# Constant products on TensorE in the first tiles, and a start that is loaded and converted in pieces

## The chip, the cores and the metric

The kernel runs on one core of one Trainium2 chip. The metric is the device time of one execution in microseconds (us), and the profile is that of one execution taken by the hardware profiler. The engines are called PE (TensorE), DVE (VectorE), ACT (ScalarE), POOL (GpSimd) and SP (SyncE, which here only issues transfers).

## What is computed

An attention whose scores are cut off close to each row's maximum feeds a chain of matrix products, whose result feeds a mixture of eight experts. Sizes: 4 batches x 8 heads, 576 tokens, 64 per head; 2304 tokens of 512 features; inner width 1024. The four weights of the middle part arrive as 64-bit floats.

```python
scores = scale * np.matmul(q, k.transpose(0, 1, 3, 2))
thresh = np.max(scores, axis=-1, keepdims=True) - tau
scores = np.where(scores >= thresh, scores, -1000000000.0)
attn = np.exp(scores - np.max(scores, axis=-1, keepdims=True))
attn = attn / (np.sum(attn, axis=-1, keepdims=True) + 1e-09)
x = np.matmul(attn, v)
...
h = (x @ w1) * (x @ w2) @ w3
x = h @ w_out
...
for e in range(E):
    out += P[:, e:e + 1] * (np.maximum(x @ w1[e], 0.0) @ w2[e])
```

## The kernel before, in words

The order of the instructions on each engine is written out by hand; there is no scheduler. `attention` walks over 16 pairs of heads with nine tiles of 128 query rows each, so 144 tiles, and a step `s` of its main loop does one stage of several tiles. The letters of `ORDER = "mSTqelVoyifgsrRcxtXvwz"` name the stages in the order in which a step writes them: `m` the mask of tile s (DVE, L160), `S` the scores of tile s+2 (PE, L140), `T` and `e` the transposes of tile s-1 and their way out of PSUM (PE L185, ACT L190), `q` and `l` the same for the tails of three tiles (L196, L201), `r` and `R` the preparation of the next pair of heads, `c` and `z` the conversion of 64-bit weights, `x`, `t` and `X` row maximum (DVE L145), threshold (ACT L148) and exponential (ACT L153) of tile s+2, `v` the products with the values for tile s-5 (PE L227), `y` and `i` their scaling and the reciprocals (DVE), `V` and `o` the transposes back and the copies into x for the group of s-10, `w` products of `w3` and `w_out`, and `f` the copy of a finished block of those (ACT L437, `w34o`) with its store.

The scores have two buffers (`bufs=2` in `scores`). So the scores of tile s+2 wait for the mask of tile s, the mask waits for the exponential, and that waits for the row maximum.

Queries and keys are split in two parts for exact products: `kh` (ACT, L116) and the rest `kl` (DVE or POOL, L119), `qs` (ACT L108, lower half finished by DVE L112). The pieces of a pair of heads are named by `prep(n, part)`. Head 0 of pair 0 is done ahead of the loop, and `PREP` gives the steps of the later pairs.

`W34` converts the 40 chunks of 64-bit weights in four pieces each (`to_f32`, DVE L455 to L463, POOL L464 and L465). A step takes 2 pieces for s < RAMP = 4 and `CONVERT[s % 18]` pieces later, and `mms` issues up to `PRODUCTS[s % 18]` of the 192 products of converted chunks per step, once their chunks are there.

The second half of the kernel, `Moe`, is opened in the first step from 144 on in which all 192 products are done and copied out:

```python
if s >= NT and k.moe is None and fill.done():
    early.close()
    k.moe = Moe(k)
```

Its tiles take the memory that `early.close()` gives back, so its first instructions wait until the last store of `w34o` has read it. They sum and split x (DVE L590 and L598, ACT L597) and load and split the first weights (SP L526, POOL L543 to L555); a DVE instruction `u` (L636) is the first that needs sums of the new products.

Of the kernel before, what the change touches and what calls it, by code (L numbers as in the profile page):

```python
# [9 lines left out]
F32 = mybir.dt.float32  # L10
F32R = mybir.dt.float32r
AF = mybir.ActivationFunctionType
ALU = mybir.AluOpType
# [6 lines left out]
B, H, S, D = 4, 8, 576, 64  # L20
DM, DFF, E = 512, 1024, 8
NTOK = B * S
NP = B * H // 2
# [10 lines left out]
CONVERT = (1, 1, 1, 1, 1, 1, 1, 1, 0, 1, 1, 2, 2, 1, 1, 2, 1, 1)  # L34
# [2 lines left out]
PREP = {1: (0, 4), 2: (2, 1), 4: (3,), 5: (6,), 7: (8, 5), 8: (9, 7)}  # L37
PD = 2
SHARE = 2.0
RAMP = 4  # L40
CHUNKS = "oowoooo33o3o33ww3ww3333wwww3w33w3ww3ww3w"


def f32(ap):
    return ap.bitcast(F32)
# [6 lines left out]
def attention(k):  # L52

    tc, nc = k.tc, k.nc
    early, late = ExitStack(), ExitStack()
    pool = late.enter_context(tc.tile_pool(name="att", bufs=1, side="right"))
    psum = late.enter_context(tc.tile_pool(name="attp", bufs=1, space=bass.MemoryType.PSUM, side="right"))
    epool = early.enter_context(tc.tile_pool(name="atte", bufs=1))
    psums = early.enter_context(tc.tile_pool(name="atts", bufs=1, space=bass.MemoryType.PSUM))

    k.ident = pool.tile([128, 128], F32, name="ident")
    make_identity(nc, k.ident)
    NT = 9 * NP
    last = pool.tile([128, 65], F32, name="last")
# [3 lines left out]
    thr = pool.tile([128, 18], F32, name="thr")  # L68
# [4 lines left out]
    raws, sets = {}, {}  # L73

    def load(n, i):
        if n >= NP:
            return
        t = epool.tile([128, 2, S], F32, tag=f"r{i}", name=f"r{i}_{n}", bufs=2)
        raws[n, i] = t
        if n:  # L80
            fetch(n, i, slice(0, 2))

    def fetch(n, i, h):
        for half in range(2):
            nc.sync.dma_start(raws[n, i][64 * half:64 * half + 64, h], k.qk[n, :, 2 * i + h.start:2 * i + h.stop])

    def load_v(n):
        if n >= NP:
            return
        rv = pool.tile([128, 2, 5, D], F32, tag="rv", name=f"rv{n}", bufs=2)  # L90
        nc.sync.dma_start(rv, k.vv[n])
        raws["v", n] = rv

    def prep(n, part):
        if n >= NP:
            return
        rq, rk = raws[n, 0], raws[n, 1]
        if n not in sets:
            qs = epool.tile([128, QW], F32R, tag="qs", name=f"qs{n}", bufs=2)
            kh = epool.tile([128, 2, S], F32R, tag="kh", name=f"kh{n}", bufs=2)  # L100
            kl = epool.tile([128, 2, S], F32R, tag="kl", name=f"kl{n}", bufs=2)
            sets[n] = (qs, kh, kl)
            nc.gpsimd.memset(f32(qs[:, S:S + 128]), 0.0)
        qs, kh, kl = sets[n]
        qcol = (slice(0, S), slice(S + 128, QW))
        if part in (0, 1):
            h = part
            nc.scalar.activation(qs[:, qcol[h]], rq[:, h], AF.Copy, scale=0.125)  # L108
        elif part in (2, 3, 8, 9):
            h, o = part % 2, 0 if part < 4 else 288  # L110
            dst = qs[64:128, qcol[h].start + o:qcol[h].start + o + 288]
            nc.vector.scalar_tensor_tensor(  # L112
                out=dst, in0=rq[64:128, h, o:o + 288], scalar=0.125, in1=f32(dst), op0=ALU.mult, op1=ALU.subtract)
        elif part in (4, 5):
            h = part - 4
            nc.scalar.activation(kh[:, h], rk[:, h], AF.Copy)  # L116
        elif part in (6, 7):
            h = part - 6
            (nc.gpsimd if n or h else nc.vector).tensor_tensor(out=kl[:, h], in0=rk[:, h], in1=f32(kh[:, h]), op=ALU.subtract)  # L119

    spool, ppool, tpool, outs = {}, {}, {}, {}

    def scores(s):
        if s >= NT:
            return
        n, t = divmod(s, 9)
        qs, kh, kl = sets[n]
        ps = psums.tile([128, 2, 512], F32, tag="s", name=f"s{s}", bufs=2)
        spool[s] = ps
        if t == 4:  # L130
            todo = [(512, 0), (640, 1)]
        elif t < 4:
            todo = [(128 * t, 0)]
        else:
            todo = [(QW - S + 64 + 128 * (t - 5), 1)]
        for c in range(2):
            cols = slice(288 * c, 288 * c + 288)
            ops = [(q0, h, kk) for q0, h in todo for kk in (kh, kl)]
            for i, (q0, h, kk) in enumerate(ops):
                nc.tensor.matmul(ps[:, c, 0:288], lhsT=qs[:, q0:q0 + 128], rhs=kk[:, h, cols],  # L140
                                 start=i == 0, stop=i == len(ops) - 1)

    def rowmax(s):
        ps = spool[s]
        nc.vector.tensor_reduce(out=nmx[:, s % 18:s % 18 + 1], in_=ps[:, :, 0:288], axis=AX.XY, op=ALU.max, negate=True)  # L145

    def thresh(s):
        nc.scalar.activation(thr[:, s % 18:s % 18 + 1], nmx[:, s % 18:s % 18 + 1], AF.Identity, bias=k.ntau, scale=-1.0)  # L148

    def expo(s):  # L150
        e = pool.tile([128, 2, 288], F32, tag="e", name=f"e{s}", bufs=2)
        spool[s] = (spool[s], e)
        nc.scalar.activation(e, spool[s][0][:, :, 0:288], AF.Exp, bias=nmx[:, s % 18:s % 18 + 1], scale=1.0)  # L153

    def mask(s):
        ps, e = spool.pop(s)
        g, i = divmod(s, 3)
        if i == 0:
            ppool[g] = pool.tile([128, 3, S + 4], F32, tag="p", name=f"p{g}", bufs=3)
        nc.vector.scalar_tensor_tensor(out=ppool[g][:, i, 0:S].rearrange("p (a b) -> p a b", a=2), in0=ps[:, :, 0:288],  # L160
                                       scalar=thr[:, s % 18:s % 18 + 1], in1=e, op0=ALU.is_ge, op1=ALU.mult,
                                       accum_out=ssum[:, s % 18:s % 18 + 1])
# [40 lines left out]
    def vsum(n):  # L203

        rv = raws["v", n]
        ps = psum.tile([128, 512], F32, tag="tt", name=f"vs{n}", bufs=1)
        for i in range(5):
            r = 128 if i < 4 else 64
            nc.tensor.matmul(ps[0:65, 0:128], lhsT=last[0:r], rhs=rv[0:r, :, i], start=i == 0, stop=i == 4)
        nc.scalar.activation(rv[64:65, :, 4], ps[64:65, 0:128].rearrange("p (a b) -> p a b", a=2), AF.Copy)  # L210
# [39 lines left out]

    load(0, 1)
    load(0, 0)
    for h in range(2):
        fetch(0, 1, slice(h, h + 1))
        fetch(0, 0, slice(h, h + 1))
    nc.sync.dma_start(k.ntau, k.tau.to_broadcast([128, 1]))
    nc.scalar.activation(thr[:, 0:1], k.ident[:, 0:1], AF.Exp)
    fill = W34(k, epool, psum)
    load(1, 0)
    load(1, 1)  # L260
    for part in (4, 6, 0, 2):
        prep(0, part)
    nc.scalar.mul(k.ntau, k.ntau, -1.0)
    load_v(0)
    scores(0)
    scores(1)
    for s in range(2):
        rowmax(s)
        thresh(s)
        expo(s)  # L270
    prep(0, 8)
    prep(0, 5)
    prep(0, 7)

    def parts(s, which):
        n, t = divmod(s, 9)
        for part in PREP.get(t, ())[which]:
            prep(n + 1, part)

    def tiles(f, d):  # L280

        return lambda s: f(s - d) if 0 <= s - d < NT else None

    def groups(f, d):

        return lambda s: f((s - d) // 3) if (s - d) % 3 == 0 and 0 <= s - d < NT else None

    steps = {
        "m": tiles(mask, 0), "S": tiles(scores, -2), "x": tiles(rowmax, -2), "t": tiles(thresh, -2), "X": tiles(expo, -2),
        "T": tiles(transp, 1), "e": tiles(evac, 1), "g": groups(flags, 1), "s": groups(sums, 3), "i": groups(inverse, 5),  # L290
        "q": groups(tails, 3), "l": groups(tail_out, 3), "v": tiles(pv, 5), "y": groups(scale, 8),
        "V": groups(back, 10), "o": groups(x_out, 10), "f": lambda s: fill.out(),
        "c": lambda s: fill.convert(s, 2 if s < RAMP else CONVERT[s % 18]), "z": lambda s: fill.convert(s, 0),
        "r": lambda s: parts(s, slice(0, 1)), "R": lambda s: parts(s, slice(1, 9)), "w": lambda s: fill.mms(s)}
    ahead = iter(())
    for s in range(NT + 19):
        n, t = divmod(s, 9)
# [3 lines that stand above are left out]
            ahead = k.moe.run()  # L301
        for what in ORDER:
            if what in steps:
                steps[what](s)
        if s < 2:
            for part in ((1, 3), (9,))[s]:
                prep(0, part)
        if n < NP and t in (2, 4):
            load(n + 2, t // 2 - 1)
        if n < NP and t == 2:  # L310
            vsum(n)
        if n < NP and t == 6:
            load_v(n + 1)
        if k.moe:
            next(ahead)
# [618 lines left out]
```

## Time and profile before

| | before |
|---|---|
| median of 3 timed runs | 2296.33 us (2295.28 to 2297.43) |
| the profiled execution, device time | 2291.91 us |
| its span, first to last instruction | 2290.1 us |
| PE busy | 2228.0 us, 97% of the span |
| DVE, ACT, POOL busy | 1261.5, 971.5, 1055.0 us |

The device time of the profiled execution is 1.8 us above its span, and the median of the timed runs lies 4.4 us above it. Starts in the rows are microseconds from the start of the span. Of each row of a timeline the columns are: start, duration, engine, line, operation, output<-inputs, shapes, number of merged instructions, and in brackets the idle time ahead of it with what ended it.

### The profile page before, as it was taken

How to read it: one execution, taken by the hardware profiler on the slowest of the kernel's cores; microseconds unless marked ns; L12 is line 12 of the kernel's file. 1: busy time of each engine (PE TensorE's matmuls, PEld its weight loads, DVE VectorE, ACT ScalarE, POOL GpSimd, SP SyncE). 2: the span in 40 equal slices, each digit the busy share in tenths (PEclk: the TensorE clock that was granted, in tenths of full speed). 3: DMA queues.
4: the chain of work that ended last, by engine and by line, in shares of the span. 5: the costliest groups of instructions: out<-in, count | busy, mean ns of one | idle time of the engine just before them, and what ended most of it. 6: DMA issues, size and time to landing. Idle time of an engine off the chain costs nothing.

```text
span 2290.1 us, 32049 instructions
## 1 busy us (share of the span) xinstructions
PE 2228.0 (97%) x12544; PEld 2034.3 (89%) x12544; DVE 1261.5 (55%) x2207; ACT 971.5 (42%) x1805; POOL 1055.0 (46%) x997
## 2 busy tenths in 40 slices
PE   6999999989999999999999999999999999999999
PEld 5899999888989888999999999999999999999998
DVE  7888888665554555544444634444445544444444
ACT  6877877643222433333333433333333343333332
POOL 4654555385110444444455644444445544444442
PEclk9999999989999999999999999999999999999999
DMA  5434443165444212112212212212212212211211
GB/s 144 119 104 123 130 122 118 50 243 206 151 168 174 78 56 74 66 64 74 71 59 74 102 56 74 74 56 74 74 56 74 102 57 72 74 63 68 74 67 44
DMA packets 57432, 213.37 MB, mean 93 GB/s; under 512 B 7105, under 2 KB 7105, under 8 KB 57281
## 3 DMA queue, kind: packets, MB, share of 16 engines
q1 hardware_dynamic: 57280, 211.33, 27.0%
q8 instruction: 98, 1.61, 0.3%
q14 instruction: 54, 0.43, 0.1%
HBM read 185.61 MB, written 25.69 MB: 92 GB/s over the span
## 4 chain that ended last, share of the span: by engine, by line
PE 69%; DVE 1%; issue 0%; ACT 0%; POOL 0%; DVEq 0%; ACTq 0%
PE ye L679 36%; PE py L609 19%; PE px L609 14%; DVE xl L598 0%; PE py L758 0%; DVE c L653 0%; PE px L758 0%; DVE c L664 0%; DVE prob L796 0%; ACT xh L597 0%; DVE acc L733 0%; POOL w1l L553 0%; DVE hl L675 0%; POOL w1l L550 0%; DVE small L793 0%
## 5 line engine op out<-in xcount | busy, mean ns | idle before, releaser
L679 PE MATMUL ye<-w2h,hl 128*128 128x512 f32 x1152 | 452.0, 392 | 0.0
L679 PE MATMUL ye<-w2h,hh 128*128 128x512 f32 x1152 | 451.4, 392 | 0.0
L679 PE MATMUL ye<-w2l,hh 128*128 128x512 f32 x1152 | 450.5, 391 | 0.0
L674 ACT ACTIVATE hh<-c 128x384 fp32r<-128x384 f32 x288 | 151.4, 526 | 611.4 <-DVE c L653 611.3
L555 POOL TENSOR_TENSOR w1l<-wt,w1h 128x1024 fp32r<-128x1024 f32 x104 | 251.7, 2420 | 286.4 <-ACT w1h L552 286.4
L609 PE MATMUL py<-xh,w1h 128*128 128x384 f32 x960 | 323.7, 337 | 8.4 <-DVE c L653 3.6
L609 PE MATMUL py<-xl,w1h 128*128 128x384 f32 x960 | 323.0, 336 | 3.5 <-DVE xl L598 3.5
L609 PE MATMUL py<-xh,w1l 128*128 128x384 f32 x960 | 322.0, 335 | 0.4 <-POOL w1l L555 0.4
L550 POOL TENSOR_TENSOR w1l<-raw,w1h 128x256 fp32r<-128x256 f32 x104 | 79.4, 764 | 479.0 <-ACT w1h L544 463.7
L609 PE MATMUL px<-xh,w1h 128*128 128x384 f32 x720 | 242.8, 337 | 5.5 <-ACT p L633 2.8
L679 PEld LDWEIGHTS ye<-w2l,hh 128*128 128x128 f32 x1152 | 216.3, 188 | 32.4
L679 PEld LDWEIGHTS ye<-w2h,hl 128*128 128x128 f32 x1152 | 216.2, 188 | 32.4
L609 PE MATMUL px<-xl,w1h 128*128 128x384 f32 x720 | 242.2, 336 | 2.7 <-DVE xl L598 2.7
L609 PE MATMUL px<-xh,w1l 128*128 128x384 f32 x720 | 242.1, 336 | 0.0
L679 PEld LDWEIGHTS ye<-w2h,hh 128*128 128x128 f32 x1152 | 216.3, 188 | 24.1 <-ACT x L705 0.2
L609 PEld LDWEIGHTS py<-xh,w1h 128*128 128x128 f32 x960 | 180.4, 188 | 33.1 <-DVE c L653 6.4
L609 PEld LDWEIGHTS py<-xl,w1h 128*128 128x128 f32 x960 | 180.3, 188 | 23.2 <-DVE xl L598 5.3
L636 DVE TENSOR_TENSOR u<-py,p 128x384 f32<-128x384 f32 x120 | 66.7, 556 | 216.0 <-PE py L609 212.1
L609 PEld LDWEIGHTS py<-xh,w1l 128*128 128x128 f32 x960 | 180.3, 188 | 0.9 <-POOL w1l L555 0.9
L543 POOL TENSOR_TENSOR wt<-raw 128x512 f32<-128x512 f32 x104 | 140.5, 1351 | 87.2 <-DMA raw<-in_e 61.0
L675 DVE SCALAR_TENSOR_TENSOR hl<-c,hh 128x384 fp32r<-128x384 f32 x288 | 165.1, 573 | 9.3
L674 ACT ACTIVATE hh<-px 128x384 fp32r<-128x384 f32 x96 | 47.2, 492 | 272.5 <-PE px L609 272.5
(138 smaller groups left out, 4393.9 us busy)
## 6 DMA issues: line engine op xcount, KB each, us to landing
raw<-in_e SPq DMA_DIRECT2D x192, 512.0 KB, 4.0
r<-in_qk SPq DMA_DIRECT2D x60, 288.0 KB, 5.8
wraw<-in_w SPq DMA_DIRECT2D x32, 512.0 KB, 4.0
w1h<-w_kept SPq DMA_DIRECT2D x16, 896.0 KB, 4.9
w1l<-w_kept SPq DMA_DIRECT2D x16, 896.0 KB, 6.8
w_kept<-w1h SPq DMA_DIRECT2D x8, 896.0 KB, 7.3
w_kept<-w1l SPq DMA_DIRECT2D x8, 896.0 KB, 8.2
raw<-w SPq DMA_DIRECT2D x12, 512.0 KB, 3.5
```

The costliest lines, as they stand in the source:

```text
L543: nc.gpsimd.tensor_tensor(out=t[:, 0:2], in0=raw[:, 1:3], in1=raw[:, 0:2], op=ALU.subtract)
L550: nc.gpsimd.tensor_tensor(out=wl[:, 0], in0=raw[:, 0], in1=f32(wh[:, 0]), op=ALU.subtract)
L555: nc.gpsimd.tensor_tensor(out=wl[:, 3:7], in0=t, in1=f32(wh[:, 3:7]), op=ALU.subtract)
L609: self.nc.tensor.matmul(out, lhsT=w[:, wi, o], rhs=x[xi][:, d], start=n == 0 and not adds, stop=n == 5, skip_group_check=True)
L636: tt(out=self.u2, in0=py, in1=self.p1, op=ALU.add)
L674: nc.scalar.activation(hi, src, AF.Relu)
L675: self.later.append(lambda: nc.vector.scalar_tensor_tensor(out=lo, in0=src, scalar=0.0, in1=f32(hi), op0=ALU.max, op1=ALU.subtract))
L679: self.queue.append((out.shape[-1], lambda: self.nc.tensor.matmul(out, lhsT=l, rhs=r, start=start, stop=stop, skip_group_check=True)))
```

## The change

A tile `hot` of ones is set by DVE, and `busy(n)` issues n products of 128x512 from it, written to the PSUM buffer that the `w34` products use later. They stand ahead of the first scores (9), behind the scores of tile 1 (7), and at the end of the steps 0 to 11 (1, 5, 6, 6, 5, 4, 4, 3, 3, 2, 2, 2): 59 in all, whose results nobody reads. The first head's keys and queries are loaded in smaller pieces, two of them issued by ACT, and split in halves. The masks of tiles 0 and 1 stand both in step 0, and the second head of pair 0 is prepared ahead of the first conversions. No pieces are converted in the steps 0 and 1, and two in each of the steps 2 to 5.

```diff
--- before.py
+++ after.py
@@ -37,7 +37,8 @@
 PREP = {1: (0, 4), 2: (2, 1), 4: (3,), 5: (6,), 7: (8, 5), 8: (9, 7)}
 PD = 2
 SHARE = 2.0
-RAMP = 4
+RAMP = 6
+BUSY = (1, 5, 6, 6, 5, 4, 4, 3, 3, 2, 2, 2)
 CHUNKS = "oowoooo33o3o33ww3ww3333wwww3w33w3ww3ww3w"
 
 
@@ -59,6 +60,8 @@
     psums = early.enter_context(tc.tile_pool(name="atts", bufs=1, space=bass.MemoryType.PSUM))
 
     k.ident = pool.tile([128, 128], F32, name="ident")
+    hot = epool.tile([128, 128], F32R, name="hot")
+    nc.vector.memset(f32(hot), 1.0)
     make_identity(nc, k.ident)
     NT = 9 * NP
     last = pool.tile([128, 65], F32, name="last")
@@ -91,17 +94,21 @@
         nc.sync.dma_start(rv, k.vv[n])
         raws["v", n] = rv
 
-    def prep(n, part):
-        if n >= NP:
-            return
-        rq, rk = raws[n, 0], raws[n, 1]
+    def operands(n):
+
         if n not in sets:
             qs = epool.tile([128, QW], F32R, tag="qs", name=f"qs{n}", bufs=2)
             kh = epool.tile([128, 2, S], F32R, tag="kh", name=f"kh{n}", bufs=2)
             kl = epool.tile([128, 2, S], F32R, tag="kl", name=f"kl{n}", bufs=2)
             sets[n] = (qs, kh, kl)
             nc.gpsimd.memset(f32(qs[:, S:S + 128]), 0.0)
-        qs, kh, kl = sets[n]
+        return sets[n]
+
+    def prep(n, part):
+        if n >= NP:
+            return
+        rq, rk = raws[n, 0], raws[n, 1]
+        qs, kh, kl = operands(n)
         qcol = (slice(0, S), slice(S + 128, QW))
         if part in (0, 1):
             h = part
@@ -119,6 +126,13 @@
             (nc.gpsimd if n or h else nc.vector).tensor_tensor(out=kl[:, h], in0=rk[:, h], in1=f32(kh[:, h]), op=ALU.subtract)
 
     spool, ppool, tpool, outs = {}, {}, {}, {}
+
+    def busy(n):
+
+        if n:
+            ps = psum.tile([128, 4, 128], F32, tag="w34", name="hot", bufs=1)
+        for i in range(n):
+            nc.tensor.matmul(ps, lhsT=hot, rhs=hot.unsqueeze(1).to_broadcast([128, 4, 128]), start=True, stop=True)
 
     def scores(s):
         if s >= NT:
@@ -250,27 +264,43 @@
 
     load(0, 1)
     load(0, 0)
-    for h in range(2):
-        fetch(0, 1, slice(h, h + 1))
-        fetch(0, 0, slice(h, h + 1))
+    rk, rq = raws[0, 1], raws[0, 0]
+    both = ((nc.sync, slice(0, 64)), (nc.scalar, slice(64, 128)))
+    for eng, half in both:
+        eng.dma_start(rk[half, 0:1], k.qk[0, :, 2:3])
+    for eng, half in both:
+        eng.dma_start(rq[half, 0, 0:288], k.qk[0, :, 0, 0:288])
+    for half in (slice(0, 64), slice(64, 128)):
+        nc.sync.dma_start(rq[half, 0, 288:S], k.qk[0, :, 0, 288:S])
     nc.sync.dma_start(k.ntau, k.tau.to_broadcast([128, 1]))
-    nc.scalar.activation(thr[:, 0:1], k.ident[:, 0:1], AF.Exp)
+    for i in (1, 0):
+        fetch(0, i, slice(1, 2))
+    nc.scalar.activation(thr[:, 0:1], f32(hot)[:, 0:1], AF.Exp)
     fill = W34(k, epool, psum)
     load(1, 0)
     load(1, 1)
-    for part in (4, 6, 0, 2):
-        prep(0, part)
+    busy(9)
+    qs, kh, kl = operands(0)
+    nc.scalar.activation(kh[:, 0], rk[:, 0], AF.Copy)
+    nc.scalar.activation(qs[:, 0:288], rq[:, 0, 0:288], AF.Copy, scale=0.125)
+    nc.vector.tensor_tensor(out=kl[:, 0, 0:288], in0=rk[:, 0, 0:288], in1=f32(kh[:, 0, 0:288]), op=ALU.subtract)
+    prep(0, 2)
+    nc.vector.tensor_tensor(out=kl[:, 0, 288:S], in0=rk[:, 0, 288:S], in1=f32(kh[:, 0, 288:S]), op=ALU.subtract)
+    nc.scalar.activation(qs[:, 288:S], rq[:, 0, 288:S], AF.Copy, scale=0.125)
     nc.scalar.mul(k.ntau, k.ntau, -1.0)
     load_v(0)
     scores(0)
     scores(1)
-    for s in range(2):
-        rowmax(s)
-        thresh(s)
-        expo(s)
+    busy(7)
     prep(0, 8)
-    prep(0, 5)
-    prep(0, 7)
+    rowmax(0)
+    expo(0)
+    thresh(0)
+    rowmax(1)
+    expo(1)
+    thresh(1)
+    for part in (5, 7, 1):
+        prep(0, part)
 
     def parts(s, which):
         n, t = divmod(s, 9)
@@ -286,11 +316,11 @@
         return lambda s: f((s - d) // 3) if (s - d) % 3 == 0 and 0 <= s - d < NT else None
 
     steps = {
-        "m": tiles(mask, 0), "S": tiles(scores, -2), "x": tiles(rowmax, -2), "t": tiles(thresh, -2), "X": tiles(expo, -2),
+        "m": lambda s: [mask(i) for i in ((0, 1) if s == 0 else () if s == 1 or s >= NT else (s,))], "S": tiles(scores, -2), "x": tiles(rowmax, -2), "t": tiles(thresh, -2), "X": tiles(expo, -2),
         "T": tiles(transp, 1), "e": tiles(evac, 1), "g": groups(flags, 1), "s": groups(sums, 3), "i": groups(inverse, 5),
         "q": groups(tails, 3), "l": groups(tail_out, 3), "v": tiles(pv, 5), "y": groups(scale, 8),
         "V": groups(back, 10), "o": groups(x_out, 10), "f": lambda s: fill.out(),
-        "c": lambda s: fill.convert(s, 2 if s < RAMP else CONVERT[s % 18]), "z": lambda s: fill.convert(s, 0),
+        "c": lambda s: fill.convert(s, (0, 0, 2, 2, 2, 2)[s] if s < RAMP else CONVERT[s % 18]), "z": lambda s: fill.convert(s, 0),
         "r": lambda s: parts(s, slice(0, 1)), "R": lambda s: parts(s, slice(1, 9)), "w": lambda s: fill.mms(s)}
     ahead = iter(())
     for s in range(NT + 19):
@@ -302,9 +332,12 @@
         for what in ORDER:
             if what in steps:
                 steps[what](s)
-        if s < 2:
-            for part in ((1, 3), (9,))[s]:
-                prep(0, part)
+        if s < len(BUSY):
+            busy(BUSY[s])
+        if s == 0:
+            prep(0, 3)
+        elif s == 1:
+            prep(0, 9)
         if n < NP and t in (2, 4):
             load(n + 2, t // 2 - 1)
         if n < NP and t == 2:
```

On ACT, at the end of step 0 and in step 1, the rows before are these (`kh0`, `qs0` are the second head of pair 0, `qs1`, `kh1` the first head of pair 1, `cvq`, `cvl` the conversion, `pt0` the transposes of tile 0 on their way out):

```order
L116 ACTIVATE kh0_118<-r1_0_93 128x576
L453 ACTIVATE cvq_158<-wraw0_107 128x512
L454 ACTIVATE cvl_159<-wraw0_107 128x512
L148 ACTIVATE thr_89<-nmx_88,ntau_62 128x1
L153 ACTIVATE e2_166<-s2_151,nmx_88 128x576
L108 ACTIVATE qs0_117<-r0_0_94 128x576
L190 ACTIVATE pt0_184<-t0_179 128x512
L108 ACTIVATE qs1_189<-r0_1_111 128x576
L116 ACTIVATE kh1_190<-r1_1_114 128x576
L148 ACTIVATE thr_89<-nmx_88,ntau_62 128x1
L153 ACTIVATE e3_198<-s3_174,nmx_88 128x576
```

And in the changed kernel:

```order
L123 ACTIVATE kh0_132<-r1_0_95 128x576
L115 ACTIVATE qs0_131<-r0_0_96 128x576
L162 ACTIVATE thr_91<-nmx_90,ntau_62 128x1
L167 ACTIVATE e2_184<-s2_177,nmx_90 128x576
L204 ACTIVATE pt0_199<-t0_194 128x512
L115 ACTIVATE qs1_204<-r0_1_115 128x576
L123 ACTIVATE kh1_205<-r1_1_118 128x576
L162 ACTIVATE thr_91<-nmx_90,ntau_62 128x1
L167 ACTIVATE e3_212<-s3_189,nmx_90 128x576
```

The conversion has left this place and `qs0` stands earlier; `qs1` and `kh1`, which need the second pair's load, still stand ahead of the threshold and the exponential of tile 3.

On PE, the steps 2 to 4 before (`t` transposes, `vs0` the sums over the values, `tt0` tails; runs of equal rows are merged):

```order
L185 MATMUL t1_214<-ident_80,p0_149 128x128 x4
L209 MATMUL vs0_243<-rv0_126,last_85 65x128 x5
L140 MATMUL s5_252<-kh0_118,qs0_117 128x288
L140 MATMUL s5_252<-kl0_119,qs0_117 128x288
L140 MATMUL s5_252<-kh0_118,qs0_117 128x288
L140 MATMUL s5_252<-kl0_119,qs0_117 128x288
L185 MATMUL t2_257<-ident_80,p0_149 128x128 x4
L196 MATMUL tt0_262<-ident_80,p0_149 65x128 x3
L140 MATMUL s6_280<-kh0_118,qs0_117 128x288
```

And in the changed kernel:

```order
L199 MATMUL t1_231<-ident_80,p0_174 128x128 x4
L135 MATMUL hot_255<-hot_81 128x512 x6
L223 MATMUL vs0_265<-rv0_142,last_87 65x128 x5
L154 MATMUL s5_274<-kh0_132,qs0_131 128x288
L154 MATMUL s5_274<-kl0_133,qs0_131 128x288
L154 MATMUL s5_274<-kh0_132,qs0_131 128x288
L154 MATMUL s5_274<-kl0_133,qs0_131 128x288
L199 MATMUL t2_279<-ident_80,p0_174 128x128 x4
L210 MATMUL tt0_284<-ident_80,p0_174 65x128 x3
L135 MATMUL hot_301<-hot_81 128x512 x6
L154 MATMUL s6_309<-kh0_132,qs0_131 128x288
```

Six constant products stand between one tile's transposes and the next tile's scores, in each of these steps.

On PE, from the last products of step 143 on, before (`w34_7` the last block of products, `pv` products with the values, `xt` transposes back):

```order
L426 MATMUL w34_7_5253<-wol_106,w3h38_5512 128x512
L426 MATMUL w34_7_5253<-woh_105,w3l38_5513 128x512
L185 MATMUL t143_5660<-ident_80,p47_5583 128x128 x4
L196 MATMUL tt47_5665<-ident_80,p47_5583 65x128 x3
L227 MATMUL pv46_5652<-rv15_5292,pt139_5565 128x2x64 x4
L227 MATMUL pv46_5652<-rv15_5292,ptt46_5601 128x2x64
L241 MATMUL xt45_5714<-ident_80,xo45_5649 64x128 x3
L227 MATMUL pv46_5652<-rv15_5292,pt140_5599 128x64 x4
L227 MATMUL pv46_5652<-rv15_5292,ptt46_5601 128x64
L227 MATMUL pv47_5735<-rv15_5292,pt141_5623 128x64 x4
```

And in the changed kernel:

```order
L199 MATMUL t143_5737<-ident_80,p47_5654 128x128 x4
L210 MATMUL tt47_5742<-ident_80,p47_5654 65x128 x3
...
L241 MATMUL pv46_5728<-rv15_5363,pt140_5670 128x64 x4
L241 MATMUL pv46_5728<-rv15_5363,ptt46_5672 128x64
L459 MATMUL w34_7_5358<-wol_110,w3h38_5639 128x512
L241 MATMUL pv47_5771<-rv15_5363,pt141_5698 128x64 x4
L241 MATMUL pv47_5771<-rv15_5363,ptt47_5748 128x64
L241 MATMUL pv47_5771<-rv15_5363,pt142_5722 128x64 x4
L241 MATMUL pv47_5771<-rv15_5363,ptt47_5748 128x64
L459 MATMUL w34_7_5358<-woh_109,w3l38_5640 128x512
L255 MATMUL xt46_5783<-ident_80,xo46_5767 64x128 x4
```

The last two of the 192 products have moved from step 143, ahead of the transposes of tile 143, to the steps 145 and 147. The copy `w34o` stands in the step after the last product, and `Moe` opens in the step after that: step 145 before, step 149 now.

## Rows read from the trace of the kernel before

**Rows 1.** Windows: stretch, length, busy us of PE, PEld, DVE, ACT, POOL; clock; DMA share; GB/s.

```profile
10.00:18.00 8.00, 2.84 (x11) 2.54 (x12) 4.96 (x11) 4.34 (x9) 2.35 (x5) 1.00 1.02 277
100.00:400.00 300.00, 292.66 (x2280) 274.99 (x2280) 251.18 (x526) 234.95 (x500) 163.99 (x232) 1.00 0.41 121
```

**Rows 2.** Timeline of PE: starts of scores (s) and sums (vs), tiles 3 to 13.

```profile
16.46 0.58 PE L140 MATMUL s<-kh,qs 128*128 128x288 f32 x1 [3.80 <-DVE p L160]
...
17.55 1.05 PE L185 MATMUL t<-ident,p 128*128 128x128 f32 x4
20.36 0.58 PE L140 MATMUL s<-kh,qs 128*128 128x288 f32 x1 [1.75 <-DVE p L160]
...
23.26 2.38 PE L209 MATMUL vs<-rv,last 128*65 128x128 f32 x10
25.58 0.40 PE L140 MATMUL s<-kh,qs 128*128 128x288 f32 x1
...
31.97 0.44 PE L140 MATMUL s<-kh,qs 128*128 128x288 f32 x1 [2.44 <-DVE p L160]
...
49.17 0.40 PE L140 MATMUL s<-kh,qs 128*128 128x288 f32 x1
```

**Rows 3.** Timeline of PE, the step from the scores of tile 8 to those of tile 9.

```profile
35.69 0.38 PE L140 MATMUL s<-kh,qs 128*128 128x288 f32 x1
...
37.06 1.00 PE L227 MATMUL pv<-rv,pt 128*128 128x64 f32 x8
...
38.10 0.38 PE L140 MATMUL s<-kh,qs 128*128 128x288 f32 x1
```

**Rows 4.** Timeline of DVE: the mask of tile 1, a conversion pass in step 2.

```profile
15.49 0.82 DVE L160 SCALAR_TENSOR_TENSOR p<-s,thr,e 128x576 f32<-128x576 f32 x1
...
20.85 1.40 DVE L455 TENSOR_SCALAR cva<-wraw 128x512 int32<-128x512 int32 x1
```

**Rows 5.** Timeline of ACT: the second pair's keys and the exponential of tile 3.

```profile
19.71 0.67 ACT L116 ACTIVATE kh<-r 128x576 fp32r<-128x576 f32 x1
...
20.47 0.73 ACT L153 ACTIVATE e<-s,nmx 128x576 f32<-128x576 f32 x1
```

**Rows 6.** Timeline of SP: issue of the first loads (start, time of all, count).

```profile
0.72 5.04 SPq L85 DMA_DIRECT2D r<-in_qk  x8
...
7.38 2.39 SPq L85 DMA_DIRECT2D r<-in_qk  x4
9.81 0.58 SPq L91 DMA_DIRECT2D rv<-in_vv  x1
```

**Rows 7.** DMA issues from 9.15 to 9.9: operation, count, KB, us to landing.

```profile
rv<-in_vv SPq DMA_DIRECT2D x1, 320.0 KB, 9.2
r<-in_qk SPq DMA_DIRECT2D x1, 288.0 KB, 9.0
```

**Rows 8.** Timeline of PE: two neighbouring products of 128x512.

```profile
416.48 0.39 PE L426 MATMUL w<-wol,w3h 128*128 128x512 f32 x1
416.71 0.39 PE L426 MATMUL w<-woh,w3l 128*128 128x512 f32 x1
```

**Rows 9.** Timeline of PE from the transposes of tile 143 on.

```profile
451.57 0.60 PE L185 MATMUL t<-ident,p 128*128 128x128 f32 x4
...
453.78 1.00 PE L227 MATMUL pv<-rv,pt 128*128 128x64 f32 x8
...
458.42 1.53 PE L227 MATMUL pv<-rv,pt 128*128 128x64 f32 x8 [3.41 <-DVE rin L179]
```

**Rows 10.** Timeline of ACT where the second half opens.

```profile
453.07 0.59 ACT L437 ACTIVATE w34o<-w 128x512 f32<-128x512 f32 x1
...
455.91 0.84 ACT L597 ACTIVATE xh<-x 128x768 fp32r<-128x768 f32 x1 [1.44 <-DMA w<-w34o]
```

**Rows 11.** Timeline of DVE where the second half opens.

```profile
457.79 0.48 DVE L234 TENSOR_TENSOR xo<-pv,rin 128x128 f32<-128x128 f32 x2
...
474.08 0.54 DVE L636 TENSOR_TENSOR u<-py,p 128x384 f32<-128x384 f32 x1
```

## The prediction

> **What bounds the kernel now.** I read the page first, then the windows by stage, then the timelines of the first 55 us and of the stretch from 440 to 480 us. From 100 to 400 us PE is busy 292.7 of 300 us, DVE 251.2 [rows 1]: the attention is bound by PE there, and a tile that comes earlier or later at 50 us stays so up to step 143. After the opening of the second half the instructions of before and after stand in the same order on all engines. So the change can act in two places only: the first 14 tiles, and the opening.
>
> In the first tiles PE waits. The scores of tile 3 start at 16.46 after 3.80 us of idle time that DVE's mask ended, those of tile 7 at 31.97 after 2.44 us [rows 2]. [...] At the opening a serial chain runs: copy `w34o` at 453.07, its store, first split of x at 455.91 [rows 10], and `u` at 474.08 [rows 11], while PE waits.
>
> **The first tiles, step by step.** The eight loads of the first pair took SP 5.04 us, 0.63 each [rows 6]. With ACT issuing a half, the first keys lie 0.6 us earlier, and splitting in halves adds perhaps as much again. [...] I put tile 0 at 1.4 us earlier; the next gate makes the exact figure unimportant.
>
> The mask of tile 1 started at 15.49 [rows 4] behind two conversion passes, a row maximum and a head's split, and the scores of tile 3 followed 0.97 us behind it [rows 2]. It now stands right behind the mask of tile 0, so tile 3 can start at about 10 and tile 4 at 13.5 instead of 20.36 [rows 2]: 6 to 7 us gained, for the moment.
>
> What is late next is a load. `qs1` and `kh1` stand on ACT ahead of the exponential of tile 3, and `kh1` needs the last of four transfers that SP issued from 7.38 on: issued at 9.2, landed 9.0 us later, at 18.2 [rows 6, 7]. Before, `kh1` started at 19.71 [rows 5], so nobody saw it. SP issues sixteen loads up to `rv0` in both kernels, and the 16 engines were fully busy (share 1.02) from 10 to 18 us [rows 1], so I leave 18.2. From the start of `kh1` to the end of the exponential is 20.47 + 0.73 - 19.71 = 1.49 us [rows 5]: exponential done at 19.75, mask, and the scores of tile 5 at 19.75 + 0.97 = 20.7. Ahead of them on PE stands `vs0`, whose load was issued at 9.81 and took 9.2 us [rows 6, 7], to 19.0. The scores of tile 4 (two heads, 1.1), transposes (0.4) and six constant products (1.4) from 13.5 on are done by 16.5, so PE is idle for 2.5 us. I take the low clock after that, as after the 2.44 us ahead of 31.97 (the first scores there last 0.44, against 0.38 at 35.69) [rows 2, 3]: `vs0` then takes 2.32 (23.26 to 25.58) [rows 2], and tile 5 starts at 21.4, against 25.58: 4.2 us earlier.
>
> [...]
>
> Step 3: scores, transposes and tails took 37.06 - 35.69 = 1.37 us at the high clock [rows 3], some 2.5 at the low one; with six constant products, by then mostly fast (at 35.69, 3.7 us after 31.97, the clock was back [rows 2, 3]), 6 x 0.23 = 1.4. Tile 6 starts at 25.3. Step 4 has five more, but its mask comes later than they do: the conversion moved here has a pass of up to 1.40 us beside POOL [rows 4], then row maximum, second pass and mask, 3.2 us in all: tile 7 at 28.5, against 31.97.
>
> From here PE is the bound. A step without waits is 38.10 - 35.69 = 2.41 us [rows 3], and the steps 5 to 10 add 4 + 4 + 3 + 3 + 2 + 2 = 18 products, 4.1 us: tile 13 at 28.5 + 14.5 + 4.1 = 47.1, against 49.17. The 2.41 holds tail transposes that only two of the six steps have, so tile 13 may come up to 1 us sooner; two products more in step 11 cost 0.5. **The gain that reaches the steady part is about 2 us**, out of 7 at tile 4. Bounds: 0.3 if all products of the steps 3 and 4 run slowly; 4.5 if the load lands 2 us earlier and the clock stays high.
>
> The split halves, the memset of `hot` and the earlier second head cost nothing by themselves: ACT and DVE wait for the loads meanwhile; without that cover they are some 0.5 us. The moved conversions are as many as before in all, two of them later.
>
> **The opening, step by step.** Two pieces fewer are converted in the first steps, and the last chunk is ready a step later. Two of the 192 products miss step 143 and fall into 145 and 147, where `PRODUCTS` allows one each. So `w34o` moves from step 144 to 148.
>
> Counted from the transposes of tile 143 (451.57), the last `pv46` starts at 2.21 and takes 38.10 - 37.06 = 1.04 [rows 3, 9]; one product 0.23; the scaling `xo` 0.48 [rows 11] beside it, so `pv47` at about 4.0; two of these 2.08; the last product 0.23; transposes 0.60; two copies into x about 0.7: `w34o` at about 7.65, against 453.07 - 451.57 = 1.50 [rows 10]: 6.15 later. The transposes themselves come 0.46 earlier, since two products have left. From `w34o` on the chain is as before, 474.08 - 453.07 = 21.0 us, except that the scalings and reciprocal of the last groups, some 0.75 us of DVE's chain, are done ahead of it; before, they were stuck in it, and PE waited 3.41 us for the reciprocal [rows 9]. **The opening costs 6.15 - 0.46 - 0.75 = 5 us.** Bounds: 4, if more of DVE's and POOL's contention goes; 6.2, if none of the 0.75 returns and PE stays longer at the low clock.
>
> **The sum.** -2 + 5 = +3 us on a profiled execution of 2291.9 (span 2290.1 + 1.8), so 2295; and the same +3 on the median of 2296.33, which lies 4.4 above that execution: 2299.4. By the bounds it is -0.5 to +6. A difference of 0.2%, 4.6 us, is about what can be told from none.
>
> **Rivals.**
> Slower by more than that: the constant products run at the low clock behind the wait for `rv0`. They stand ahead of the scores of tiles 6 and 7 in PE's order, 11 in all, and at twice 0.23 they add 2.5 us, with slow scores and transposes 1 us more; the gain then is below zero and the time 2302 to 2303. It decides from the point where more than six of the eleven are slow. For it: the low clock from 16.46 to 25.58 although PE worked most of the time from 20.36 on [rows 2]; against: the return 3.7 us after 31.97.
>
> Faster: the constant products cost nothing, since DVE and not PE sets the pace up to tile 13 (a pass of 1.40 us is in rows 4). Then 18 + 2 products, 4.6 us, come back and the gain is 6.6: 2294.8, within 0.2%; more only if the loads land sooner too. Against: the step of 2.41 us has no wait in it, and transposes of tile 0, whose mask stands ahead of that of 15.49, ran at 17.55 behind waiting scores [rows 2, 4]: PE takes its products in order.
>
> The opening doesn't move the time: if the chain from `w34o` to `u` were gated by the attention's last tiles. Then 2294.3. Against: the first split waited for the store of `w34o`, after 1.44 us of idle time [rows 10].
>
> **How the numbers follow.** My forecast 0.57, slow products 0.22, free products 0.13, free opening 0.08. The forecast's own range is 2296 to 2302.3, the slow rival begins at 2301 and the fast ones end at 2294; with the timed runs' own 1 us the range is 2294.3 to 2303. A quarter of the chance lies above 2300.9 (most of the slow rival, the upper end of the forecast), 0.07 below 2291.7 (both fast rivals at once, or a load that lands far earlier).
>
> **What would show it.** Right: ACT idle until about 18 ahead of `kh1`, ended by a DMA; tile 5 at 20.5 to 21.5; constant products with no wait behind them from tile 7 on; tile 14 2 us earlier than before; `w34o` 6 us later behind the transposes of tile 143, and `u` 21 - 0.75 us behind it. Wrong: PE waiting ahead of the scores in steps 6 to 10, exponential of tile 3 before 17, or the first split of x ended by something other than the store.

## The result and the profile after

| | before | after |
|---|---|---|
| median of 6 timed runs | 2295.60 us (2292.92 to 2297.43) | 2311.89 us (2309.52 to 2313.51) |
| span of the profiled execution | 2290.1 us | 2309.8 us |

The changed kernel takes 1.0071 times as long (95% interval 1.0060 to 1.0081): 16.3 us more, where 3 were forecast, and outside the forecast's range. The profiled executions lie 19.7 us apart, and not 16.3, since the one before is faster than all six of its timed runs; in which stage is not known. Differences to that execution therefore come out 2 to 7 us above those of the times. Between the changed kernel and e1, an experiment below, times and profiles agree: 20.9 and 21.2 us.

The timeline of PE after, with `vs0` and the scores of tiles 5, 7, 13, 14 and 143, answers to [rows 2]:

```profile
19.04 1.45 PE L223 MATMUL vs<-rv,last 128*65 128x128 f32 x10 [1.85 <-DMA rv<-in_vv]
...
20.75 0.40 PE L154 MATMUL s<-kh,qs 128*128 128x288 f32 x1 [0.26 <-DVE p L174]
...
28.41 0.40 PE L154 MATMUL s<-kh,qs 128*128 128x288 f32 x1 [1.12 <-DVE p L174]
...
46.40 0.29 PE L154 MATMUL s<-kh,qs 128*128 128x288 f32 x1
...
50.80 0.40 PE L154 MATMUL s<-kh,qs 128*128 128x288 f32 x1
...
455.64 0.40 PE L154 MATMUL s<-kh,qs 128*128 128x288 f32 x1 [0.57 <-DVE p L174]
```

Tiles 14 and 143 before:

```profile
53.17 0.40 PE L140 MATMUL s<-kh,qs 128*128 128x288 f32 x1
...
443.77 0.40 PE L140 MATMUL s<-kh,qs 128*128 128x288 f32 x1
```

The first tiles are as the prediction has them: tile 5 at 20.75, tile 13 at 46.40 against 49.17 before, tile 14 (50.80) 2.4 us earlier than before. What the prediction took as settled is lost behind them, and not in one place: against before, tile 14 starts 2.4 us earlier, tile 41 is 1.8 us late, tile 77 5.0 and tile 113 10.3. The window of after, for [rows 1]:

```profile
100.00:400.00 300.00, 287.03 (x2212) 264.92 (x2210) 262.66 (x507) 232.52 (x487) 160.47 (x227) 1.00 0.40 116
```

In the same 300 us PE works through 2212 instructions in place of 2280, and DVE is busy 11.5 us longer with 19 fewer. PE's waits for a mask in this stretch (us in all, how many, the longest), before and after:

```profile
PE s L140 <- DVE p L160: 4.7, 12, 0.4
```

```profile
PE s L154 <- DVE p L174: 8.9, 22, 0.8
```

So the longer work on DVE reaches PE: the masks come late. From tile 14 to tile 143 PE is idle 21.7 us after and 11.8 before, and 4.3 us more are counted as busy for nearly the same instructions; where those 4.3 come from was not traced.

The groups of DVE by line, from 53 to 440 us, say which instructions grew (busy us, mean ns). Before:

```profile
L160 DVE SCALAR_TENSOR_TENSOR p<-s,thr,e 128x576 f32<-128x576 f32 x128 | 103.6, 809 | 2.0 <-ACT e L153 1.5
L145 DVE TENSOR_REDUCE nmx<-s 128x1 f32<-128x576 f32 x128 | 96.6, 755 | 46.7 <-PE s L140 45.9
L112 DVE SCALAR_TENSOR_TENSOR qs<-r,qs 64x288 fp32r<-64x288 f32 x55 | 26.0, 473 | 1.5
L461 DVE SCALAR_TENSOR_TENSOR cvq<-cvq,cva 128x512 f32<-128x512 f32 x36 | 24.8, 690 | 0.8
```

After:

```profile
L174 DVE SCALAR_TENSOR_TENSOR p<-s,thr,e 128x576 f32<-128x576 f32 x124 | 100.1, 807 | 1.1 <-ACT e L167 0.9
L159 DVE TENSOR_REDUCE nmx<-s 128x1 f32<-128x576 f32 x123 | 92.7, 753 | 32.5 <-PE s L154 31.4
L119 DVE SCALAR_TENSOR_TENSOR qs<-r,qs 64x288 fp32r<-64x288 f32 x55 | 39.9, 725 | 1.5
L494 DVE SCALAR_TENSOR_TENSOR cvq<-cvq,cva 128x512 f32<-128x512 f32 x34 | 31.5, 926 | 0.7
```

The masks and row maxima, which read the scores from PSUM, last as long as before. The second half of a split of q went from 473 to 725 ns, the third conversion pass from 690 to 926. What they wait for is seen with POOL and DVE side by side, after, from 208 to 213 us. POOL:

```profile
208.09 1.28 POOL L408 TENSOR_TENSOR w3l<-wf,w3h 128x512 fp32r<-128x512 f32 x1 [2.60 <-ACT w3h L407]
209.33 1.42 POOL L126 TENSOR_TENSOR kl<-r,kh 128x576 fp32r<-128x576 f32 x1
```

DVE:

```profile
208.12 0.76 DVE L159 TENSOR_REDUCE nmx<-s 128x1 f32<-128x576 f32 x1
208.91 0.82 DVE L174 SCALAR_TENSOR_TENSOR p<-s,thr,e 128x576 f32<-128x576 f32 x1
...
209.65 1.65 DVE L494 SCALAR_TENSOR_TENSOR cvq<-cvq,cva 128x512 f32<-128x512 f32 x1
211.22 0.75 DVE L159 TENSOR_REDUCE nmx<-s 128x1 f32<-128x576 f32 x1
```

Where POOL's passes are narrow (e13, below) `cvq` takes 0.69 us. Here it begins 0.32 us into POOL's `kl` and ends 0.55 us after the end of `kl` (210.75). The row maximum and the mask beside `w3l`, at 208.12 and 208.91, are not held up; the next row maximum comes straight behind `cvq`, at 211.22.

The opening after: PE's transposes of tile 143, ACT's copy and first split, DVE's `u`, for [rows 9 to 11].

```profile
463.90 0.60 PE L199 MATMUL t<-ident,p 128*128 128x128 f32 x4
```

```profile
471.87 0.60 ACT L470 ACTIVATE w34o<-w 128x512 f32<-128x512 f32 x1
474.59 0.84 ACT L630 ACTIVATE xh<-x 128x768 fp32r<-128x768 f32 x1 [2.12 <-DMA w<-w34o]
```

```profile
492.51 0.54 DVE L669 TENSOR_TENSOR u<-py,p 128x384 f32<-128x384 f32 x1
```

`w34o` stands 7.97 us behind these transposes (1.50 before), and `u` 20.64 us behind `w34o` (21.01 before).

Two measures carry the rest: the time from the scores of tile 14 to those of tile 143 (**pace**), and from there to `u` (**opening**), each read from the starts shown above and in [rows 11]. The 19.7 us are then: start -2.4, pace +14.2 (404.84 against 390.60), opening +6.6 (36.87 against 30.31), and +1.3 from `u` to the end.

### The profile page after: what moved, and what is told of

The parts are those of the page before. It is cut to its first block, busy times and chain, and to the rows that moved or that the text cites. A ratio compares the mean times of both kernels' runs of the same rounds, so it can differ in the third digit from the quotient of the medians.

```text
span 2309.8 us, 32203 instructions
## 1 busy us (share of the span) xinstructions
PE 2241.6 (97%) x12603; PEld 2037.8 (88%) x12603; DVE 1290.2 (56%) x2209; ACT 976.8 (42%) x1806; POOL 1057.7 (46%) x997
## 4 chain that ended last, share of the span: by engine, by line
PE 68%; DVE 1%; issue 0%; ACT 0%; POOL 0%; DVEq 0%; ACTq 0%
PE ye L712 35%; PE py L642 18%; PE px L642 14%; DVE xl L631 0%; PE py L791 0%; DVE c L686 0%; PE px L791 0%; DVE c L697 0%; DVE prob L829 0%; ACT xh L630 0%; DVE acc L766 0%; POOL w1l L586 0%; DVE hl L708 0%; POOL w1l L583 0%; DVE small L826 0%
```

## Experiments

In the first six steps the changed kernel takes up eight conversion pieces, where the one before takes ten; called below by that number. From step 6 on both follow the same table, two of a chunk's four pieces apart. Six of the kernels (e7, e9 and e12 to e15) leave out most columns of some passes, to price these, and so compute something else. Each kernel is timed against the kernel before on the same chip; pace, opening and the start of tile 14 are differences to before in the profiled executions (us).

| kernel | us (before) | pace | opening | tile 14 |
|---|---|---|---|---|
| after (8 pieces) | 2311.9 (2295.6) | +14.2 | +6.6 | -2.4 |
| e1: 10 | 2291.0 (2294.5) | 0.0 | -0.2 | -1.0 |
| e2: before with 8 | 2318.1 (2294.5) | +14.2 | +6.5 | +6.9 |
| e3: 8, no constant products | 2310.0 (2294.5) | +14.2 | +6.6 | +0.5 |
| e4: 10, none after step 4 | 2289.5 (2294.5) | -0.1 | -0.2 | -2.1 |
| e5: 12 | 2307.7 (2295.8) | +15.2 | -2.8 | +1.6 |
| e6: 6 | 2297.4 (2295.8) | -1.0 | +8.0 | -0.6 |
| e7: 8, conversions narrow on POOL | 2303.3 (2295.8) | +6.7 | +6.6 | -3.3 |
| e8: 7 | 2306.3 (2295.8) | +9.1 | +7.1 | -2.1 |
| e9: 10, as e7 | 2287.2 (2294.5) | -3.1 | -0.2 | +0.3 |
| e10: 10, no constant products | 2291.4 (2294.5) | 0.0 | -0.2 | -0.8 |
| e11: 14, none after step 4 | 2293.5 (2294.5) | +3.4 | -3.3 | +2.8 |
| e12: 8, all POOL narrow | 2291.6 (2296.0) | -5.6 | +6.6 | -2.2 |
| e13: 10, as e12 | 2285.2 (2296.0) | -5.3 | -0.2 | -0.8 |
| e14: 8, DVE conversions narrow | 2297.2 (2296.0) | +1.4 | +6.2 | -3.1 |
| e15: 10, as e14 | 2284.2 (2296.0) | -6.2 | -0.3 | +0.1 |

**Which part of the change?** Four kernels. e1 gives the changed kernel its two pieces back:

```diff
-fill.convert(s, (0, 0, 2, 2, 2, 2)[s] if s < RAMP else ...)
+fill.convert(s, (0, 0, 2, 2, 3, 3)[s] if s < RAMP else ...)
```

> The changed kernel with all its other parts, but ten conversion pieces by step 7 as in the kernel before (it had two fewer from step 5 on). From step 8 on every engine's order is that of the kernel before. Theory A, the lag of two pieces slows the tiles 14 to 143 (about 14 us) and delays the last products (about 6): 2291 to 2296 us, the steps of tiles take as long as before, and tile 143 starts about 2.4 us earlier than before. Rival B, the constant products or the new start do lasting harm (the clock, or what they leave behind): it stays at 2308 to 2313. Rival C, the lag costs only the later products and the start costs the tiles: about 2305.

e2 takes two from the kernel before:

```diff
-RAMP = 4
+RAMP = 6
-fill.convert(s, 2 if s < RAMP else ...)
+fill.convert(s, (0, 0, 2, 2, 2, 2)[s] if s < RAMP else ...)
```

> The kernel before with one edit: two conversion pieces fewer in steps 0 to 5, so eight in place of ten; no constant products, the old start. From step 11 on every engine's order is that of the changed kernel. Theory A: slower than the changed kernel by the start's gain, 2312 to 2317 us, with the splits of q on VectorE at about 0.72 us in place of 0.47. Rival B: 2294 to 2297, as before. Rival C: about 2301, with the loss in the opening alone.

e3 empties the loop over constant products:

```diff
-        for i in range(n):
+        for i in range(0):
```

> The changed kernel without its 59 constant products (the lag of two pieces stays). Theory A: 2306 to 2315 us, tiles 14 to 143 as slow as in the changed kernel; the products' own worth, the clock against 20 of them on TensorE's path in steps 5 to 11, is what is left of the difference, at most 4 us either way. Rival B: about 2296.

e4 is e1 with this:

```diff
-BUSY = (1, 5, 6, 6, 5, 4, 4, 3, 3, 2, 2, 2)
+BUSY = (1, 5, 6, 6, 5)
```

> As the first of these kernels (ten pieces by step 7), and without the 20 constant products of steps 5 to 11. If TensorE is the bound in those steps, they cost 20 x 0.215 = 4.3 us: 2287 to 2292. Rival: they keep the clock high; without them it falls before step 12 and the gain is lost: 2293 to 2297.

Measured: ratios 0.9981 (0.9972 to 0.9989), 1.0090 (1.0077 to 1.0104), 1.0065 (1.0053 to 1.0078) and 0.9977 (0.9966 to 0.9987). Theory A holds in the first three: the pace of 14.2 us goes and comes with the two pieces, with the new start or the old, with constant products or without. e1 lies at the lower edge of its range, and tile 143 starts 1.0 us earlier than before, not 2.4: the two pieces given back cost the first tiles 1.4 us. The splits of q, by line from 53 to 440 us in e1 and in e2:

```profile
L119 DVE SCALAR_TENSOR_TENSOR qs<-r,qs 64x288 fp32r<-64x288 f32 x55 | 26.0, 473 | 1.5
```

```profile
L112 DVE SCALAR_TENSOR_TENSOR qs<-r,qs 64x288 fp32r<-64x288 f32 x54 | 39.3, 728 | 1.5
```

e2 came 1 us above its range: it also lost 6.9 us by tile 14, nearly all of it between the tiles 6 and 12; this part was not tried by itself. e4 lies within its own range and is faster than both kernels, but only 1.5 us under e1, not 4.3, and the intervals of the two overlap: the 20 products did not stand on the path with their full length. The 0.215 us for each is an estimate that no row shows; two neighbours start 0.23 us apart [rows 8].

**Position or lateness?** Three more counts, edited in the same tuple.

```diff
-(0, 0, 2, 2, 2, 2)
+(0, 2, 2, 2, 3, 3)   # e5, twelve
+(0, 0, 1, 1, 2, 2)   # e6, six
+(0, 0, 2, 2, 2, 1)   # e8, seven
```

> The changed kernel with twelve conversion pieces by step 7: two ahead of the kernel before where the changed kernel is two behind. A chunk has four pieces, so two ahead puts the same piece of a chunk on the same step as two behind. Theory A1, what counts is which piece falls beside the head preparation: tiles 14 to 143 lose 10 to 14 us as in the changed kernel, the opening loses nothing: 2301 to 2307 us. Rival A2, what counts is that pieces come late: 2288 to 2293, no slower than with ten.

> The changed kernel with six pieces by step 7: four behind the kernel before, one whole chunk, so each step has the same piece as before, of one chunk earlier. Theory A1: tile 143 starts as early as with ten pieces (443 us), and only the opening is later, by 6 to 10 us: 2296 to 2302. Rival A2 (lateness): slower than the changed kernel, over 2315, with tile 143 after 460.

> The changed kernel with seven pieces by step 5, three behind. Theory A1 gives no order by size: the tiles' loss is that of another phase, anything from 0 to 14 us, and must not lie on a line through 0 at ten pieces and 14 at eight; the opening is 6 to 10 later, so 2297 to 2314. Rival A2 (lateness): tiles lose about 21 us, over 2318.

Measured 1.0048 (1.0033 to 1.0063), 1.0007 (0.9997 to 1.0016) and 1.0043 (1.0028 to 1.0058). Two pieces early cost as much pace as two late, a whole chunk late costs none, and seven pieces cost less than eight: it is which piece falls on which step. (e5 came 0.7 us above its range.) e6 also prices the opening by itself: 8.0 us for four pieces by the profiles, with the tiles as fast as before.

**Whose passes?** e7 and e9 leave GpSimd's two conversion passes, with eight and with ten pieces, 64 of 512 columns; the low words of the others are left out.

```diff
-    nc.scalar.activation(lf, low.bitcast(U32), AF.Copy, scale=2.0 ** -52)
+    nc.scalar.activation(out, low.bitcast(U32), AF.Copy, scale=2.0 ** -52)
...
-    nc.gpsimd.tensor_tensor(out=lf, in0=lf, in1=f32(sm), op=ALU.mult)
-    nc.gpsimd.tensor_tensor(out=out, in0=lf, in1=sq, op=ALU.add)
+    part = out[:, 0:64]
+    nc.gpsimd.tensor_tensor(out=part, in0=part, in1=f32(sm[:, 0:64]), op=ALU.mult)
+    nc.gpsimd.tensor_tensor(out=part, in0=part, in1=sq[:, 0:64], op=ALU.add)
```

> The changed kernel (eight pieces) with GpSimd's two conversion passes on 64 columns in place of 512: this leaves out the low words of the other 448 columns. The number and order of instructions stay. Theory A1 by GpSimd's passes: VectorE's splits of q fall back from 0.72 to near 0.47 us and tiles 14 to 143 regain 8 to 14 us: 2297 to 2304, with the opening as late as in the changed kernel. Rival A3, it is the order of VectorE's and ScalarE's own pieces, whatever GpSimd does: 2308 to 2313.

> Ten pieces, with GpSimd's two conversion passes on 64 of 512 columns (the low words of the other 448 are left out). With eight pieces the narrow passes gave back 8 us. Theory A1 (these passes cost time only where they stand beside VectorE's passes of two inputs from SBUF): with ten pieces they give back 0 to 2 us, 2289 to 2291. Rival A3, narrow passes are worth 8 us in any order: 2282 to 2285.

Measured 1.0030 (1.0020 to 1.0040) and 0.9969 (0.9957 to 0.9980). e7 met its range, but e9 missed: the narrow passes were worth 3.8 us against e1, not 0 to 2. By pace, eight pieces still lose 6.7 + 3.1 = 9.8 us against ten, of 14.2: the two passes are the smaller part. In e7 the splits of q are back at 465 ns, as expected, but the second and third conversion passes take 872 and 860 ns (709 and 690 before): not the splits alone carry the loss. So the remaining wide passes were taken out as well. e12 and e13 add, with the tiles for `kl` and `w3l` kept from one use to the next:

```diff
+            w = slice(0, 64 if n > 1 else S)
-            ...tensor_tensor(out=kl[:, h], in0=rk[:, h], in1=f32(kh[:, h]), op=ALU.subtract)
+            ...tensor_tensor(out=kl[:, h, w], in0=rk[:, h, w], in1=f32(kh[:, h, w]), op=ALU.subtract)
...
+        c = slice(0, 512 if what == "o" or self.nw3 < 4 else 64)
-        nc.gpsimd.tensor_tensor(out=lo, in0=w, in1=f32(hi), op=ALU.subtract)
+        nc.gpsimd.tensor_tensor(out=lo[:, c], in0=w[:, c], in1=f32(hi[:, c]), op=ALU.subtract)
```

> Eight pieces, with all of GpSimd's wide passes on 64 columns (the two conversion passes, and from the second pair of heads or the fourth chunk on the low halves kl and w3l: the rest of their columns is left as it was). Theory P, tiles lose because GpSimd's passes stand beside VectorE's: against the same edit at ten pieces the tiles 14 to 143 lose 0 to 3 us and only the opening 6 to 8: 2290 to 2296 us. Theory D, VectorE's own pieces stand in steps that have no room for them: the tiles still lose 6 or more: 2297 to 2303.

> Ten pieces, with all of GpSimd's wide passes on 64 columns, as the kernel beside it: the base for it. Both theories: 2282 to 2287 us, at or under the 2287 with the two conversion passes alone on 64 columns.

e14 and e15 have POOL's passes whole, and put `[:, 0:64]` on the operands of the four DVE conversion passes (the last writes into `cvq`, which POOL then reads).

> Eight pieces, with VectorE's four conversion passes on 64 columns (the other 448 columns' exponents are left out; GpSimd's passes stay at 512). Theory P: the splits of q still wait beside GpSimd's passes, and against the same edit at ten pieces the tiles 14 to 143 lose 5 us or more, the opening 6 to 8: 11 to 16 us slower than the kernel beside it. Theory D: the tiles lose 0 to 3, 6 to 10 us slower than it.

> Ten pieces, with VectorE's four conversion passes on 64 columns: the base for the kernel beside it. VectorE has some 75 us less to do in the attention; TensorE is busy 77 to 79 of 80 us there, so at most about 5 us of it come through: 2284 to 2291 us.

Measured 0.9986 (0.9976 to 0.9995) and 0.9956 (0.9941 to 0.9971) for the first pair, 1.0008 (0.9999 to 1.0017) and 0.9948 (0.9931 to 0.9964) for the second. With POOL's wide passes gone, eight pieces pace like ten (-5.6 and -5.3), though PE's products stand in the order of after; the 6.4 us between the two times are, but for the start, the opening. With DVE's conversions narrow instead, eight still lose 7.5 us of pace, 13.0 in all, and the splits of q wait as ever; e12 and e14:

```profile
L119 DVE SCALAR_TENSOR_TENSOR qs<-r,qs 64x288 fp32r<-64x288 f32 x55 | 25.4, 462 | 1.5
```

```profile
L119 DVE SCALAR_TENSOR_TENSOR qs<-r,qs 64x288 fp32r<-64x288 f32 x55 | 41.7, 759 | 1.5
```

Theory P stands: the tiles lose because POOL's wide passes lie beside DVE's passes, and how many of them do is set by the pieces' place.

**What the parts are worth.** e10 is e3 with ten pieces, e11 is e4 with `(0, 2, 2, 2, 4, 4)`, a chunk ahead.

> Ten pieces and none of the 59 constant products: what is left of the change is the loads in halves, the conversions in pieces and the order of masks and second head. With eight pieces tile 18 started 2.9 us later without the products than with them. If that is the products' worth: 2293 to 2295, a gain of about 1 us over the kernel before. Rival, their cost on TensorE's path in steps 5 to 11 (20 x 0.215 = 4.3 us) cancels what they give: 2290 to 2292.

> Fourteen pieces by step 8, a whole chunk ahead of the kernel before, and no constant products after step 4. Theory A1: the same piece of a chunk stands on each step as in the kernel before, so the tiles keep their pace; the last products come earlier, and the opening with them (2.8 us were won there with twelve): 2286 to 2289 us, faster than 2289.5 by up to 3. Rival: the four pieces more in steps 1 to 8 cost the first tiles as much or more: 2290 to 2294.

Measured 0.9987 (0.9978 to 0.9996) and 0.9994 (0.9985 to 1.0003). In both the rival of the expectation held. e10 is 0.4 us from e1, whose products keep the clock up: the 59 products give nothing on balance that the runs can tell. From 30 to 36 us the windows of e1 and of e10 show both sides:

```profile
30.00:36.00 6.00, 6.00 (x44) 5.36 (x44) 5.89 (x10) 4.21 (x10) 5.49 (x5) 1.00 0.51 146
```

```profile
30.00:36.00 6.00, 6.00 (x28) 5.80 (x28) 4.73 (x8) 1.46 (x4) 5.42 (x5) 0.50 0.62 177
```

With them the granted clock is 1.00, without them 0.50, and both fill PE; tile 14 is 0.2 us apart between e1 and e10. e11 missed its range: the opening won 3.1 us against e4 as expected, but the four pieces more cost 4.9 by tile 14, and 3.5 us of pace were lost although each step has the same piece of a chunk; its splits of q last 472 ns, as in e4. The steps then have pieces of other chunks, of other weights; that this is the reason is not shown. e4 has the lowest time of the kernels that compute everything, 2289.5 us.

## Why the prediction was wrong

**The first tiles: right.** ACT waited for the second keys until 18.34 (18.2 forecast), tiles 6, 7 and 13 came at 25.0, 28.4 and 46.4 (25.3, 28.5, 47.1), and the gain at tile 14 was 2.4 (about 2). The choice of the low clock after the wait for `vs0` was not right: PE waited 1.85 us there, not 2.5, the clock stayed up (`vs0` took 1.45 us, not 2.32), and tile 5 came at 20.75, with its mask (20.7 forecast) and not at 21.4. What a wait of 2.5 us would have done here is not shown. The prediction's 2.5 us for scores, transposes and tails at the low clock rest on no row; in e10, at a granted clock of 0.50, they took 2.62 (33.73 to 36.35). The constant products were priced too high: leaving out 20 of them gave 1.5 us in time (e4 against e1), not 4.6. Of the 1.1 us between the two at tile 14 only 0.7 came behind tile 7, where these products begin; the other 0.4 lay between the two executions before. In e4, DVE is busy 5.87 of the 6 us from 30 to 36 and PE 4.48; there DVE sets the pace for most of it, as the faster rival had it:

```profile
30.00:36.00 6.00, 4.48 (x37) 4.21 (x37) 5.87 (x11) 4.21 (x10) 5.10 (x6) 1.00 0.57 136
```

From 36 to 42 us e4's granted clock is 0.72 where that of after is 1.00; what that took back was not tried by itself.

**The steady part: the step that failed.** The prediction put the steady part at no cost: "a tile that comes earlier or later at 50 us stays so up to step 143", and "The moved conversions are as many as before in all, two of them later." This left out 14.2 us. The table of conversions repeats every 18 steps with 20 pieces, five whole chunks, so two pieces missing at the start stay missing: every later step meets a different piece of its chunk. PE at 292.7 of 300 us [rows 1] was no proof that PE alone sets the pace: 4.7 of the 7.3 idle us were waits for DVE's masks even before, and e13 and e15 gained 5 to 6 us of pace with PE's work unchanged. The hint stood in the rows: a conversion pass of 1.40 us [rows 4], whose like takes 0.43 us when POOL is narrow (e7's mean, 430 ns), and the prediction used it for one tile only.

The trace shows which passes were held up. `cvq` at 209.65 took 1.65 us and ended after `kl`, while masks and row maxima kept their 807 and 753 ns; the longest took 819 and 760. Two of the four conversion passes, `cva` from `wraw` alone and `cvs`, have one input and were held up as well: 424 and 432 ns in e13, 850 and 630 after. What sets the passes that wait beside POOL apart from those that don't was not shown.

**The opening: right in kind, too small.** Forecast 5 us; the profile has 6.6 and the times of e12 and e13 lie 6.4 apart. `w34o` came 7.97 us behind tile 143's transposes (7.65 forecast), and the chain behind it gave back 0.37 us, not 0.75. The largest miss is the transposes themselves: they come 0.46 us later behind the scores of tile 143 (8.26 against 7.80), not 0.46 earlier, since ten of the 192 products stand between the two and not eight. The end, +1.3 us behind `u`, was not traced further.

**The rivals.** The slower one named the low clock; four transposes took 0.60 us throughout the first tiles, so the clock was high and the rival wrong, although the time lay on its side. That a constant product takes twice 0.23 us [rows 8] at the low clock, on which the rival's 2.5 us rest, no row of before shows; after, the nine ahead of the first scores took 3.94 us, 0.44 each, and the six of step 3 took 1.63, with four transposes of 0.60 ahead of them. The faster one was right on DVE in the first tiles, but the time went the other way. The free opening was wrong: the first split of x waited for the store of `w34o`, as forecast.

## What to carry over

Work interleaved by a periodic table has a phase: count how many pieces each edit adds or drops before the table starts, and compare the order of two engines step by step deep in the steady part, not only where the edit stands. A busy share near one on an engine doesn't show that its neighbours have slack: look at the mean duration of one instruction form, and where it is twice its least, lay the other engine's rows beside it. Repairing the count (e1) turns 16.3 us lost into 3.5 won; dropping the constant products of steps 5 to 11 as well (e4) makes it 5.0, a difference that lies within the intervals of the two.

## What the runs showed of the hardware

Beside POOL's wide passes, two of DVE's two-input passes, the splits of q and `cvq`, of 0.46 and 0.69 us (e13), took up to 1.66 and 1.71 us (after), and two one-input conversion passes grew from means of 0.42 and 0.43 us (e13) to 0.85 and 0.63 (after); masks and row maxima, which read PSUM, did not (0.81 and 0.76 in e13, 0.81 and 0.75 after). Over an attention this is worth 14.2 us of pace by order alone (after and e2). The granted clock stayed at 1.00 over a wait of 1.85 us, with constant products around it. Without them (e10) it fell to 0.50 from 30 to 36 us, where four transposes took 1.05 us at 30.67, against 0.60 at 25.75; in the 6 us ahead of that it was 0.80 on average and PE was busy 2.18 us. The two kernels with and without the products (e1, e10) end 0.4 us apart all the same.

At the start of these traces the clock column is no guide: before, it has 1.00 from 10 to 18 us [rows 1], while the first product of the scores at 16.46 took 0.58 us and four transposes 1.05 at 17.55 [rows 2], against 0.40 at 25.58 and 0.60 at 451.57 [rows 2, 9]. There the durations tell the level: `vs0` took 1.45 us after, 2.38 before.
